# First pair of an attention kernel: k and q turned by TensorE through PSUM and copied out, where DMA transpositions stood

## The chip, the cores and the metric

One core of a Trainium2 chip runs the program alone. The metric is the device time of one execution in microseconds (us); the median of several executions is compared. TensorE is called PE below, VectorE DVE, ScalarE ACT, GpSimd POOL, and SP is the engine from whose queue every DMA of this kernel is issued.

## What is computed

```python
def _attn_ref(q, k, v):                       # 8 batches, 8 heads, 1152 rows, 64 columns
    q_pool = q.reshape(B, H, S // 2, 2, D).mean(axis=3)
    scores = scale * np.matmul(q_pool, k.transpose(0, 1, 3, 2))
    scores = scores - np.max(scores, axis=-1, keepdims=True)
    attn = np.exp(scores)
    attn = attn / (np.sum(attn, axis=-1, keepdims=True) + 1e-09)
    return np.matmul(attn, v)

def _moe_ref(x, w_in, w_out):                 # x: 4608 x 512, from the heads side by side
    h = x @ w_in                              # 512 x 2048
    g = h * np.cos(h)
    return g @ w_out                          # 2048 x 512
```

Neighbouring rows of q are averaged, attention runs over 576 pooled queries and 1152 keys a head, and its output goes through a feed-forward layer with the gate h cos(h).

## The kernel before, in words

The 64 heads are worked as 32 pairs. A pair's k is loaded, split into a high and a low float16 part side by side (`prep_k`: a cast on ACT, a subtraction on DVE for pair 0, on POOL later), and turned so that the 2 x 64 columns lie on the partitions (`transpose_k`, line 737, tile `k1`). The upper half of `k1` is copied by DMA into `k2` (`copy_k`, line 746), whose lower half is a constant. The pooled q goes the same way: its high part, written twice, is `q1s`, turned into `q1T`; its low part with the row's negative maximum beside it is `qs2`, turned into `q2T`. Scores are two matmuls each, `k1` with `q1T` and `k2` with `q2T`, so the maximum has to be known first: the main passes (`first_main` for pair 0, `head_main` for pairs 1 and 2, `mx_main` later) are matmuls whose only use is a DVE reduction to row maxima, `mxs`.

Pair 0 has steps of its own, `first_pair`: k in two halves of 9 blocks (one a head), q in two parts of 4 and 6 blocks of 128 columns (lines 1012 to 1020), eight main passes of 1024 columns, four for each head, the rests, then `first_q2` for each half: reduce to the maximum `m` (line 990), write it into `qs2` on ACT (line 991), turn 4 or 5 blocks (line 994). After that the score units begin (`s_unit`, line 1217, in the PSUM tile `st`), each with an exponential on ACT (line 1267, tile `pp`) and a product with v on PE (line 1342 for the first pairs).

Beside the pairs run the weights of the feed-forward layer: 16 slices, each loaded, decoded on DVE by three instructions of 1024 columns (lines 518, 521, 524), squared and scaled on ACT and split on POOL. The feed-forward matmuls (line 1553) can begin once the first eight slices are done and the first batch's attention output is there; from then on they fill PE between the pairs' work.

The order on each engine is not the order of the text. `arrange` takes all recorded instructions, gives each an estimated cost and due time, plays them through and fixes one order for each engine, which the chip then executes in that order. Matmuls named `warm` (60 of 128 columns, `fillers`, line 613) do no work of the result; they are given due times by `FILL`, start, end and spacing in the planner's time, and stand between the first pair's matmuls. `marks` and `held` tie the issue of some loads behind other DMAs: pair 1's k and q and the first v behind the mark "kT", later ones behind "q2T".

Of the kernel before, what the change touches and what calls it, by code (L numbers as in the profile page):

```python
# [10 lines left out]
F16 = mybir.dt.float16  # L11
# [9 lines left out]
P = 128  # L21
# [35 lines left out]
VACT = 6  # L57
WACT = (1, 0)
HB = 2 * WACT[0]
FILL = (14.0, 26.0, 0.2)  # L60
FREM = 5
NHW = 3
HS = (-16, -15, -14, -13, -12, -10, -12, -11, -10, -9, -8, -7, -7)
# [287 lines left out]
def tile_attention_ffn(  # L351
# [10 lines left out]
    nc = tc.nc  # L362
# [11 lines left out]
    KT = S // P  # L374
# [12 lines left out]
    HALF = (slice(0, D), slice(D, P))  # L387

    fix = ctx.enter_context(tc.tile_pool(name="fix", bufs=1))
# [3 lines left out]
    psum = ctx.enter_context(tc.tile_pool(name="psum", bufs=1, space=PSUM))  # L393

    k2 = [fix.tile([P, 2 * KT * P], F16, name=f"k2_{i}") for i in range(2)]
    qs2 = fix.tile([P, NSL, P], F16, name="qs2")
    nc.gpsimd.memset(qs2, 0.0)
    q1s = fix.tile([P, NSL + 1, 2, D], F16, name="q1s")
# [45 lines left out]
            pow2_of(dst, am)  # L444

    ident = fix.tile([P, P], BF16, name="ident")

    def make_ident():
        full = sb1.tile([P, QT * P], F32, tag="xo", name="full")[:, :P]
        nc.gpsimd.memset(full, 0.0)  # L450
        nc.gpsimd.affine_select(
            out=full,
            in_=full,
            compare_op=ALU.not_equal,
            fill=1.0,
            base=0,
            pattern=[[-1, P]],
            channel_multiplier=1,
        )
        nc.scalar.copy(ident, full)  # L460

    make_ident()

    def spread(dst, mx):
# [10 lines left out]
    marks = {}  # L475
# [134 lines left out]
    def fillers():  # L610
        t = psum.tile([P, 512], F32, tag="avb", name="warm")
        for k in range(int((FILL[1] - FILL[0]) / FILL[2])):
            mm = nc.tensor.matmul(
                t[:, 0:P], ident, ident, start=True, stop=True, skip_group_check=True
            )
            fill[mm.ins.name] = FILL[0] + FILL[2] * k

# [5 lines left out]
    k1 = [fix.tile([P, 2 * KT * P], F16, name=f"k1_{i}") for i in range(3)]  # L623
# [24 lines left out]
    kst, kld, qld, q1T, q2T, vld, vam, mxs = {}, {}, {}, {}, {}, {}, {}, {}  # L648
# [8 lines left out]
    def qs2_of(n):  # L657
        return qs2b if n < NHW and n % 2 else qs2
# [28 lines left out]
    def prep_k(n, us):  # L687
        if n not in kst:
            if n in ES:
                ks = w2[0].rearrange("p f e -> p (f e)")[:, ES[n] * 2 * KW : (ES[n] + 1) * 2 * KW]  # L690
                kst[n] = ks.rearrange("p (u a d) -> p u a d", a=2, d=D)
            else:
                kst[n] = sb1.tile([P, 2 * KT, 2, D], F16, tag="kst", name="kst")
        kv, ks = kld[n][:, us], kst[n][:, us]
        nc.scalar.copy(ks[:, :, 0], kv)  # L695
        (nc.gpsimd if n else nc.vector).tensor_sub(ks[:, :, 1], kv, ks[:, :, 0])  # L696
# [20 lines left out]
    def transpose_q1(n):  # L717
        t = sb1.tile([P, NSL + 1, P], F16, tag="q1T", bufs=3, name="q1T")
        tr = nc.sync.dma_start_transpose(t, q1s.rearrange("p s a d -> p (s a d)"))
        marks.setdefault("q1T", tr)  # L720
        q1T[n] = t

    def prep_q2(n):
# [11 lines left out]
    def transpose_k(n, us):  # L735
        cs = slice(us.start * P, us.stop * P)
        tr = nc.sync.dma_start_transpose(
            k1[n % 3][:, cs].rearrange("p (u c) -> p u c", c=P),
            kst[n][:, us].rearrange("p u a d -> p (u a d)"),
        )  # L740
        if us.stop == 2 * KT:
            marks.setdefault("kT", tr)

    def copy_k(n, us=KALL):
        cs = slice(us.start * P, us.stop * P)
        nc.sync.dma_start(k2[n % 2][HALF[0], cs], k1[n % 3][HALF[0], cs])


    mx_n = [0]
# [6 lines left out]
    def mx_main(n, t, c):  # L756
        if n not in mxs:
            mxs[n] = sb2.tile([P, NSL, 3], F32, tag="mxs", name="mxs")
        mx_n[0] += 1
        two = n < NMXF and mx_n[0] % 2  # L760
        banks, m = first_tile(2, None if two else "mx")
        last = None
        for h in range(2):
            last = after(
                nc.tensor.matmul(  # L765
                    banks[h],
                    q1T[n][:, h * QT + t, :],
                    kmain(n, k1[n % 3], c, h),
                    start=True,
                    stop=True,  # L770
                    skip_group_check=True,
                ),
                last,
            )
        if two:
            for h in range(2):
                nc.vector.reduce_max(mxs[n][:, h * QT + t, c : c + 1], banks[h], axis=AX.X)
        else:
            nc.vector.reduce_max(mxs[n][:, t : t + QT + 1 : QT, c], m, axis=AX.X)  # L779
# [125 lines left out]
    def head_q2(h):  # L905
        return lambda n: n < NHW and first_q2(h, n)
# [79 lines left out]
    def first_q2(h, n=0):  # L986
        ss = slice(0, QT) if h == 0 else slice(QT, NSL)
        qq = qs2_of(n)
        m = sb2.tile([P, NSL], F32, tag="m", bufs=1, name="m")
        nc.vector.reduce_max(m[:, ss], mxs[n][:, ss], axis=AX.X)  # L990
        nc.scalar.activation(qq[:, ss, D], m[:, ss], AF.Copy, scale=-1.0 / MDIV)
        if h == 0:
            q2T[n] = sb1.tile([P, NSL, P], F16, tag="q2T", bufs=2, name="q2T")
        tr = nc.sync.dma_start_transpose(
            q2T[n][:, ss], qq[:, ss].rearrange("p s c -> p (s c)")
        )
        if h == 1:
            marks.setdefault("q2T", tr)
            mxs.pop(n)

    def first_q1(ss):
        qt = qld[0]
        qs = qt[:, ss, 0, :]
        nc.vector.tensor_add(qs, qs, qt[:, ss, 1, :])
        mains = slice(ss.start, min(ss.stop, 2 * QT))
        parts = [(slice(0, P), mains, mains)]
        for h in range(2 if ss.stop > 2 * QT else 0):
            parts.append((HALF[h], slice(2 * QT, NSL), slice(2 * QT + h, 2 * QT + h + 1)))
        for ps, a, b in parts:
            src = qt[ps, a, 0, :]  # L1010
            src = src.unsqueeze(2).broadcast_to([src.shape[0], src.shape[1], 2, D])
            nc.scalar.copy(q1s[ps, b], src)
        if ss.start == 0:
            q1T[0] = sb1.tile([P, NSL + 1, P], F16, tag="q1T", bufs=3, name="q1T")
        cs = slice(ss.start, NSL + 1 if ss.stop == NSL else ss.stop)
        tr = nc.sync.dma_start_transpose(
            q1T[0][:, cs], q1s[:, cs].rearrange("p s a d -> p (s a d)")
        )
        if ss.start:
            marks.setdefault("q1T", tr)  # L1020

    def first_low(ss):
        qt = qld[0]
# [9 lines left out]
    def first_pair():  # L1033
        k_steps(0, 0)
        first_q1(QHEAD[0])
        constants()
        first_low(QHEAD[0])
        first_q1(QHEAD[1])
        k_steps(0, 1)
        copy_k(0, KHEAD[0])  # L1040
        load_v(0)
        first_low(QHEAD[1])
        qld.pop(0)
        nc.gpsimd.memset(qs2b, 0.0)
        for t in range(QT):
            first_main(0, t, ("st", "mx")[t % 2])
        first_rest(0, "st")
        first_q2(0)
        copy_k(0, KHEAD[1])
        v_max_begin(0)  # L1050
        first_v()
        prep_v(0)
        for t in range(QT):
            first_main(1, t, ("mx", None)[t % 2])
        first_rest(1, None)
        mx_mixed(0)
        first_mixed_rest()
        first_q2(1)
# [6 lines left out]
    def transpose_q2(n):  # L1065
        t = sb1.tile([P, NSL, P], F16, tag="q2T", bufs=2, name="q2T")
        tr = nc.sync.dma_start_transpose(t, qs2.rearrange("p s c -> p (s c)"))
        marks.setdefault("q2T", tr)
        q2T[n] = t

    def load_v(n):
# [39 lines left out]
    def prep_v_lo(n, hs):  # L1111
# [3 lines left out]
        for h in hs if nf < KT else ():  # L1115
# [6 lines left out]
                ALU.subtract,  # L1122
            )

    def mains(c, ts):
        def fn(n):
            for t in ts:
                mx_main(n, t, c)

        return fn  # L1130

    def k_steps(n, part):
        us = KCUT[part] if n else KHEAD[part]
        if n == 0:
            prep_k(n, us)
        elif part == 0:
            prep_k(n, KALL)
        transpose_k(n, us)

# [4 lines left out]
        (-2, 1, pool_q),  # L1144
        (-2, 2, prep_q1),
        (-2, 2, transpose_q1),
        (-2, Q2AT, prep_q2),
        (-2, 3, lambda n: k_steps(n, 1)),
        (-2, 4, late(mains(0, (0,)))),
        (-2, 5, late(mains(0, (1,)))),  # L1150
        (-1, 2, copy_k),
        (-2, 6, late(mains(0, (2,)))),
        (-2, 7, late(mains(0, (3,)))),
# [8 lines left out]
        (-1, 3, late(mx_mixed_rest)),  # L1162
        (-1, 3, late(m_write)),
        (-1, 4, late(transpose_q2)),
        (HS[0], head_main(0, 0)),
        (HS[1], head_main(0, 1)),
# [22 lines left out]
    st = {}  # L1189
# [613 lines left out]
    for u in range(NUNITS):  # L1803
        p, i = divmod(u, NU)
# [12 lines left out]
        while credit > 0.0:  # L1817
            c = next(ffn, None)
# [74 lines left out]
```

## Time and profile before

| | |
|---|---|
| median of 3 runs | 1529.35 us (1526.34 to 1531.48) |
| the profiled execution, its own time | 1525.26 us |
| its span, first to last instruction | 1523.4 us |
| outside the span | 1.86 us |
| instructions | 39324 |

The profile's page gives the busy time of each engine over the span. The other views used below are the timeline (instructions of one engine in order of time, neighbours of one kind merged; the brackets give idle time just before and what ended it), the table by stretches (busy time of each engine within a stretch) and the table of waits (who waited for whom).

### The profile page before, as it was taken

To read this page: it belongs to the slowest core of one execution; us is meant where nothing else is said; L and a number is where in the kernel's file an instruction comes from. 1 tells how busy PE (TensorE), PEld (TensorE's weight loads), DVE (VectorE), ACT (ScalarE), POOL (GpSimd) and SP (SyncE) were. 2 spreads that over 40 slices of the span, in tenths; PEclk is the share of its full clock that TensorE was granted. 3 is DMA by queue.
4 is the path that set the end of the run, shared out by engine and by line. 5 is a ranking of instruction groups with operands and counts; after the bars stand their busy time and mean duration, and the time that the engine had idled before them with its cause. 6 is when DMAs were issued, how large, how long until landed. Compare 5 with 4: busy or idle time off the path is not lost.

```text
span 1523.4 us, 39324 instructions
## 1 busy us (share of the span) xinstructions
PE 1490.2 (98%) x16774; PEld 1027.2 (67%) x16774; DVE 1124.1 (74%) x1556; ACT 1172.4 (77%) x1475; POOL 929.6 (61%) x806
## 2 busy tenths in 40 slices
PE   5999999999999999999999999999999999999998
PEld 3777787657666676666666657667666667666665
DVE  7898987777888788887867887878787875343332
ACT  4877689888988788887968887988888787864442
POOL 4644757886665858686555586676767665521222
PEclk9999999999999999999999999999999999999999
DMA  9978742635354433535333334454453321001000
GB/s 264 273 219 181 177 93 48 125 78 116 70 102 102 108 89 76 128 79 123 73 75 79 73 83 107 86 104 103 80 120 83 80 56 32 17 19 32 20 16 22
DMA packets 226111, 145.15 MB, mean 95 GB/s; under 512 B 202448, under 2 KB 204752, under 8 KB 223888
## 3 DMA queue, kind: packets, MB, share of 16 engines
q1 hardware_dynamic: 225936, 142.65, 40.5%
q8 instruction: 131, 2.15, 0.6%
q14 instruction: 44, 0.36, 0.1%
HBM read 74.45 MB, written 10.49 MB: 56 GB/s over the span
## 4 chain that ended last, share of the span: by engine, by line
PE 88%; DVE 5%; ACT 3%; issue 1%; DMA 1%; POOL 1%; SPq 0%; ACTq 0%; DVEq 0%; POOLq 0%
PE f L1553 20%; PE f L1613 19%; PE st L1217 15%; PE ava L1293 8%; PE avb L1293 6%; PE m L765 6%; PE st L1240 2%; PE mx L1613 1%; DVE mxs L779 1%; PE ava L1342 1%; PE st L1553 1%; PE mx L808 1%; PE mx L787 1%; PE avb L1553 1%; PE mx L1553 1%
## 5 line engine op out<-in xcount | busy, mean ns | idle before, releaser
L1279 POOL TENSOR_TENSOR pp<-e,pp 128x512 f16<-128x512 f32 x374 | 457.3, 1244 | 270.6 <-ACT pp L1273 141.9
L1553 PEld LDWEIGHTS <-w 128*128 128x128 f16 x3456 | 331.4, 98 | 61.7 <-issue 3.0
L1553 PE MATMUL f<-xT,w 128*128 128x256 f16 x3048 | 366.2, 273 | 0.3 <-DVE y L1581 0.2
L1267 ACT ACTIVATE e<-st 128x1024 f32<-128x1024 f32 x267 | 272.5, 1020 | 109.9 <-PE st L1217 84.1
L779 DVE TENSOR_REDUCE mxs<-m 128x2 f32<-128x1024 f32 x232 | 283.2, 1221 | 97.1 <-PE m L765 95.0
L1613 PE MATMUL f<-w,g 128*128 128x512 f16 x1440 | 333.2, 380 | 0.7 <-DVE y L1581 0.7
L1503 POOL TENSOR_TENSOR g<-hsc,g 128x512 f16<-128x512 f32 x144 | 192.0, 1355 | 162.1 <-ACT g L1502 160.4
L1273 ACT CAST pp<-e 128x1024 f16<-128x1024 f32 x267 | 278.9, 1045 | 9.8 <-PE ava L1293 2.1
L1293 PEld LDWEIGHTS <-pp 128*128 128x128 f16 (+1 forms) x7062 | 238.8, 100 | 64.2 <-issue 12.5
L1613 PEld LDWEIGHTS <-g 128*128 128x128 f16 x1680 | 158.5, 98 | 177.3 <-DVE y L1581 0.9
L1217 PE MATMUL st<-q1T,k 128*128 128x512 f16 x576 | 218.8, 380 | 4.4 <-ACT pp L1267 4.1
L1293 PE MATMUL ava<-vc,pp 128*128 128x65 f16 (+5 forms) x4502 | 218.9, 198 | 1.3 <-DVE lx L1407 1.2
L1217 PE MATMUL st<-q2T,k 128*128 128x512 f16 x576 | 218.5, 379 | 0.0
L1293 PE MATMUL avb<-vc,pp 128*128 128x65 f16 (+1 forms) x3052 | 179.3, 197 | 0.0
L1217 PEld LDWEIGHTS <-k 128*128 128x128 f16 x1152 | 104.8, 98 | 100.9 <-issue 11.2
L1491 DVE TENSOR_TENSOR hsc<-hsc,y 128x512 f32<-128x512 f32 x144 | 134.8, 976 | 25.3 <-ACT y L1485 25.1
L1577 ACT ACTIVATE hsc<-f,small 128x512 f32<-128x512 f32 x127 | 86.7, 683 | 83.6 <-PE f L1553 83.2
L1581 DVE SCALAR_TENSOR_TENSOR y<-f,r1a,y 128x512 f32<-128x512 f32 x127 | 94.6, 745 | 66.1 <-ACT y L1580 61.3
L765 PE MATMUL m<-k,q1T 128*128 128x512 f16 x464 | 138.1, 379 | 2.5 <-DVE mxs L779 2.0
L1275 DVE TENSOR_TENSOR pp<-e,pp 128x1024 f16<-128x1024 f32 x80 | 127.5, 1593 | 16.7 <-ACT pp L1273 16.2
L1502 ACT CAST g<-hsc 128x512 f16<-128x512 f32 x144 | 83.0, 613 | 11.6 <-PE f L1613 11.6
L696 POOL TENSOR_TENSOR kst<-kld,kst 128x1152 f16<-128x1152 f32 x30 | 75.5, 2516 | 20.9 <-ACT kst L695 20.9
(189 smaller groups left out, 1853.6 us busy)
## 6 DMA issues: line engine op xcount, KB each, us to landing
vld<-in_v_dram SPq DMA_DIRECT2D x32, 576.0 KB, 3.8
kld<-in_k_dram SPq DMA_DIRECT2D x30, 576.0 KB, 4.5
qld<-in_q_dram SPq DMA_DIRECT2D x30, 576.0 KB, 4.6
k<-k SPq DMA_DIRECT2D x31, 288.0 KB, 3.5
wraw<-in_moe_w_in_dram SPq DMA_DIRECT2D x8, 1024.0 KB, 8.0
wraw<-in_moe_w_out_dram SPq DMA_DIRECT2D x8, 1024.0 KB, 6.1
out_dram<-ob SPq DMA_DIRECT2D x32, 256.0 KB, 2.4
left<-lx SPq DMA_DIRECT2D x64, 16.0 KB, 2.0
```

What stands on the lines that cost most here:

```text
L765: nc.tensor.matmul(banks[h], q1T[n][:, h * QT + t, :], kmain(n, k1[n % 3], c, h), start=True, stop=True, skip_group_check=True,),
L779: nc.vector.reduce_max(mxs[n][:, t : t + QT + 1 : QT, c], m, axis=AX.X)
L1217: nc.tensor.matmul(s[:, y, :].rearrange("p (t c) -> p t c", c=P), kcol(p, w, j, h), x[:, h * QT : (h + 1) * QT, :], start=part == 0, stop= ...
L1267: nc.scalar.activation(e, s, AF.Exp, scale=exp_scale, bias=l_add)
L1273: nc.scalar.copy(pp[:, 0, c0:n], e[:, c0:n])
L1275: nc.vector.tensor_sub(pp[:, 1, c0:n], e[:, c0:n], pp[:, 0, c0:n])
L1279: nc.gpsimd.tensor_sub(pp[:, 1, c], e[:, c], pp[:, 0, c])
L1293: mm = nc.tensor.matmul(out, w, x, start=start, stop=False, skip_group_check=True)
L1491: nc.vector.tensor_mul(hj, hj, y[:, j : j + 2])
L1503: nc.gpsimd.tensor_sub(gt[:, 1], hj, gt[:, 0])
L1553: mm = nc.tensor.matmul(ps[:, fi, :], w1[wt][:, hp, fs], ck.xT[hp][:, xi, cs], start=n == 0, stop=n == 3 * HP - 1, skip_group_check=True,)
L1613: nc.tensor.matmul(po, gt[:, gi, f % 2, ts_], w2[wt][:, f, :], start=f == 0 and (gi, wt) == (0, 0), stop=f == NF - 1 and (gi, wt) == (1, 0),)
```

## The change

Pair 0's four kinds of DMA transposition (k in two halves, q1 in two parts, q2 in two parts: 9, 9, 4, 6, 4 and 5 blocks, 37 in all) become PE transpositions of 128 columns against a float16 unit matrix `flip` into PSUM, with copies by ACT or DVE from there into the same SBUF tiles. The first half of k goes through the tile `st`, the second through two tiles `f`, q through `ava` (one tile, used four times). `KTURN` and `QTURN` say which engine copies which blocks: of k's halves ACT takes 5 blocks and DVE 4 each; of q1 DVE takes the 4 blocks and ACT the 6; of q2 DVE the 4 and ACT the 5. `FILL` begins and ends 6 earlier in the planner's time. The mark "kT" is now the first half's copy to `k2`, and "q2T" is the transposition of a later pair's q1. Later pairs keep their DMA transpositions.

```diff
-FILL = (14.0, 26.0, 0.2)
+FILL = (8.0, 20.0, 0.2)
+QTURN = (0, 1)
...
+    flip = fix.tile([P, P], F16, name="flip")
...
+        nc.scalar.copy(flip, full)
         nc.scalar.copy(ident, full)
...
     def transpose_q1(n):
...
-        marks.setdefault("q1T", tr)
+        marks.setdefault("q2T", tr)
...
-        nc.sync.dma_start(k2[n % 2][HALF[0], cs], k1[n % 3][HALF[0], cs])
+        cp = nc.sync.dma_start(k2[n % 2][HALF[0], cs], k1[n % 3][HALF[0], cs])
+        if n == 0:
+            marks.setdefault("kT", cp)
+
+    def turned(dst, src, tag, copies):
+        n = src.shape[1] // P
+        w = 2048 if tag == "st" else 1024
+        t = psum.tile([P, w], F16, tag=tag, bufs=2 if tag == "f" else 1, name="turn")
+        for i in range(n):
+            cs = slice(i * P, (i + 1) * P)
+            nc.tensor.transpose(t[:, cs], src[:, cs], flip)
+        for eng, a, b in copies:
+            cs = slice(a * P, b * P)
+            (nc.scalar.copy if eng else nc.vector.tensor_copy)(dst[:, cs], t[:, cs])
...
-        tr = nc.sync.dma_start_transpose(
-            q2T[n][:, ss], qq[:, ss].rearrange("p s c -> p (s c)")
-        )
+        src = qq[:, ss].rearrange("p s c -> p (s c)")
+        if n == 0:
+            dst = q2T[n][:, ss].rearrange("p s c -> p (s c)")
+            turned(dst, src, "ava", ((h, 0, src.shape[1] // P),))
+        else:
+            tr = nc.sync.dma_start_transpose(q2T[n][:, ss], src)
...
-        tr = nc.sync.dma_start_transpose(
-            q1T[0][:, cs], q1s[:, cs].rearrange("p s a d -> p (s a d)")
-        )
...
+        src = q1s[:, cs].rearrange("p s a d -> p (s a d)")
+        dst = q1T[0][:, cs].rearrange("p s c -> p (s c)")
+        turned(dst, src, "ava", ((QTURN[ss.start > 0], 0, src.shape[1] // P),))
...
+    KTURN = (
+        (("st", 0, KT, ((1, 0, 5), (0, 5, KT))),),
+        (("f", 0, 5, ((1, 0, 5),)), ("f", 5, KT, ((0, 0, KT - 5),))),
+    )
...
             prep_k(n, us)
-        elif part == 0:
+            for tag, a, b, copies in KTURN[part]:
+                cs = slice((us.start + a) * P, (us.start + b) * P)
+                turned(
+                    k1[0][:, cs],
+                    kst[0].rearrange("p u a d -> p (u a d)")[:, cs],
+                    tag,
+                    copies,
+                )
+            return
+        if part == 0:
             prep_k(n, KALL)
         transpose_k(n, us)
```

The planner makes new orders out of this. On DVE, from the pooling of q to the first half's maximum, this stood before (`w_1_84` is a weight slice, `m_132` to `m_152` the main passes in PSUM):

```order
L1004 TENSOR_TENSOR qld<-qld 128x5x64
L696 TENSOR_TENSOR kst<-kld,kst 128x9x64
L518 TENSOR_SCALAR w_1_84<-wraw 128x1024
L521 SCALAR_TENSOR_TENSOR w_1_84<-wraw,w_1_84 128x1024
L524 SCALAR_TENSOR_TENSOR w_1_84<-wraw,w_1_84 128x1024
L934 TENSOR_REDUCE mxs<-m_132 128x1
L934 TENSOR_REDUCE mxs<-m_137 128x1
L934 TENSOR_REDUCE mxs<-m_142 128x1
L934 TENSOR_REDUCE mxs<-m_147 128x1
L955 TENSOR_REDUCE mxs<-m_152 128x4
L990 TENSOR_REDUCE m<-mxs 128x4
```

and this stands now:

```order
L1022 TENSOR_TENSOR qld<-qld 128x5x64
L762 COPY q1T<-turn 128x512
L762 COPY k_0_94<-turn 128x512
L699 TENSOR_TENSOR kst<-kld,kst 128x9x64
L950 TENSOR_REDUCE mxs<-m_169 128x1
L762 COPY k_0_94<-turn 128x512
L950 TENSOR_REDUCE mxs<-m_174 128x1
L950 TENSOR_REDUCE mxs<-m_179 128x1
L950 TENSOR_REDUCE mxs<-m_184 128x1
L971 TENSOR_REDUCE mxs<-m_189 128x4
L1006 TENSOR_REDUCE m<-mxs 128x4
```

Three copies have come in, the third between the first and the second reduction, and the decoding of the first weight slice has left this place: it now stands behind the second half's main passes.

On PE the second main pass of the first head was followed before by one filler and the third pass; now the second half of k is turned between them, behind nine fillers and ahead of six (one row shown of each run of equal rows):

```order
L939 MATMUL m_174<-k_0_94,q1T 128x512
L616 LDWEIGHTS ident
L616 MATMUL warm<-ident 128x128
...
L759 LDWEIGHTS kst
L759 MATMUL turn<-flip,kst 128x128
...
L616 MATMUL warm<-ident 128x128
L939 LDWEIGHTS q1T
L939 MATMUL m_179<-k_0_94,q1T 128x512
```

The whole first half of k (9 blocks) and all of q1 (10 blocks) stand ahead of the first main pass.

On ACT, from the first v to the fifth exponential, this stood before:

```order
L1083 ACTIVATE vc_75,mxa<-vld 128x18x64
L695 CAST w_0_83<-w_0_83 128x18x64
L991 ACTIVATE qs_71<-m 128x4
L1106 ACTIVATE vc_75<-vld,sv 128x18x64
L712 CAST q1s<-w_0_83 128x1024
L712 CAST q1s<-w_0_83 64x128 x2
L1267 ACTIVATE pp<-st 128x1024
L991 ACTIVATE qs_71<-m 128x5
L1083 ACTIVATE vc_76,mxa<-vld 128x18x64
L1267 ACTIVATE pp<-st 128x1024
L531 ACTIVATE w_0_81,wmx<-w_1_84 128x4x256
L1267 ACTIVATE pp<-st 128x1024
```

and this stands now:

```order
L1121 ACTIVATE vc_75<-vld,sv 128x18x64
L1296 ACTIVATE pp<-st 128x1024
L715 CAST q1s<-w_0_83 128x1024
L715 CAST q1s<-w_0_83 64x128 x2
L1296 ACTIVATE pp<-st 128x1024
L1098 ACTIVATE vc_76,mxa<-vld 128x18x64
L1296 ACTIVATE pp<-st 128x1024
L1007 ACTIVATE qs_71<-m 128x5
L762 COPY q2T<-turn 128x640
L534 ACTIVATE w_0_81,wmx<-w_1_84 128x4x256
L698 CAST kst<-kld 128x18x64
L1296 ACTIVATE pp<-st 128x1024 x2
```

The first exponential (L1267, now L1296) has moved ahead of pair 1's q cast (L712, now L715), three of them now stand ahead of the second half's maximum (L991, now L1007), and the fourth stands behind a weight's square and the cast of pair 2's k.

## Rows read from the trace of the kernel before

**Rows 1.** The page, busy time of each engine over the span and its share.

```profile
PE 1490.2 (98%) x16774; PEld 1027.2 (67%) x16774; DVE 1124.1 (74%) x1556; ACT 1172.4 (77%) x1475; POOL 929.6 (61%) x806
```

**Rows 2.** The table by stretches: us, busy us and count of each engine, PEclk, DMA, GB/s.

```profile
30.00:190.00 160.00, 151.38 (x1448) 117.70 (x1448) 144.85 (x226) 115.98 (x151) 91.97 (x91) 1.00 0.83 216
190.00:1480.00 1290.00, 1283.63 (x14951) 873.32 (x14950) 948.53 (x1289) 1030.50 (x1284) 811.34 (x668) 1.00 0.36 79
```

**Rows 3.** Timeline of SP: start, us, queue, line, DMA (issue alone).

```profile
5.14 1.86 SPq L737 DMA_TRANSPOSE k<-kst  x1
...
13.46 0.57 SPq L667 DMA_DIRECT2D w<-in_k_dram  x1
...
22.06 0.39 SPq L1074 DMA_DIRECT2D vld<-in_v_dram  x1
22.90 4.30 SPq L737 DMA_TRANSPOSE k<-w  x2
27.29 1.37 SPq L719 DMA_TRANSPOSE q1T<-q1s  x1
```

**Rows 4.** Timeline of ACT, first 27 us.

```profile
5.48 0.62 ACT L1012 CAST q1s<-qld 128x512 f16<-128x512 f32 x1 [1.16 <-DVE qld L1004]
6.58 1.14 ACT L1012 CAST q1s<-qld 128x512 f16<-128x512 f32 x3 [0.48 <-DVE qld L1004]
7.74 0.67 ACT L695 CAST kst<-kld 128x576 f16<-128x576 f32 x1
...
19.27 1.15 ACT L695 CAST w<-w 128x1152 f16<-128x1152 f32 x1 [0.78 <-DMA w<-in_k_dram]
20.33 0.21 ACT L991 ACTIVATE qs<-m 128x4 f16<-128x4 f32 x1
...
26.46 1.02 ACT L1267 ACTIVATE pp<-st 128x1024 f32<-128x1024 f32 x1 [0.63 <-PE st L1217]
```

**Rows 5.** Timeline of DVE, first 33 us.

```profile
8.44 0.78 DVE L696 TENSOR_TENSOR kst<-kld,kst 128x576 f16<-128x576 f32 x1 [1.90 <-ACT kst L695]
...
13.81 3.55 DVE L934 TENSOR_REDUCE mxs<-m 128x1 f32<-128x1024 f32 x3
...
18.77 0.68 DVE L955 TENSOR_REDUCE mxs<-m 128x4 f32<-128x512 f32 x1
19.55 0.17 DVE L990 TENSOR_REDUCE m<-mxs 128x4 f32<-128x12 f32 x1
...
20.72 1.22 DVE L934 TENSOR_REDUCE mxs<-m 128x1 f32<-128x1024 f32 x1
...
27.53 0.17 DVE L990 TENSOR_REDUCE m<-mxs 128x5 f32<-128x15 f32 x1
27.61 0.70 DVE L518 TENSOR_SCALAR w<-wraw 128x1024 uint32<-128x1024 uint32 x1
...
29.61 1.23 DVE L524 SCALAR_TENSOR_TENSOR w<-wraw,w 128x1024 uint32<-128x1024 uint32 x1
32.21 1.29 DVE L867 TENSOR_REDUCE mxs<-m 128x1 f32<-128x512 f32 x2 [1.38 <-PE m L852]
```

**Rows 6.** Timeline of PE, first 32 us.

```profile
12.04 1.89 PE L923 MATMUL m<-k,q1T 128*128 128x512 f16 x4 [12.04 <-DMA q1T<-q1s]
...
15.89 0.84 PE L613 MATMUL warm<-ident 128*128 128x128 bf16 x6
...
21.13 0.67 PE L613 MATMUL warm<-ident 128*128 128x128 bf16 x9
...
28.39 1.90 PE L1342 MATMUL ava<-vc,pp 128*128 128x65 f32 x16
31.79 1.04 PE L852 MATMUL m<-k,q1T 128*128 128x512 f16 x4 [1.50 <-DMA q1T<-q1s]
```

**Rows 7.** The table of waits, 30 to 190 us, PE and DVE.

```profile
PE st L1217 <- ACT pp L1267: 3.6, 7, 1.1
...
DVE mxs L779 <- PE m L765: 4.4, 7, 1.1
```

More of the change, by code (lines that the diff above doesn't have):

```diff
@@ L993, in first_q2 @@
             q2T[n] = sb1.tile([P, NSL, P], F16, tag="q2T", bufs=2, name="q2T")
-        tr = nc.sync.dma_start_transpose(
-            q2T[n][:, ss], qq[:, ss].rearrange("p s c -> p (s c)")
-        )
+        src = qq[:, ss].rearrange("p s c -> p (s c)")
[4 more added lines that the diff above has]
+            tr = nc.sync.dma_start_transpose(q2T[n][:, ss], src)
         if h == 1:
-            marks.setdefault("q2T", tr)
             mxs.pop(n)
@@ L1015, in first_q1 @@
         cs = slice(ss.start, NSL + 1 if ss.stop == NSL else ss.stop)
-        tr = nc.sync.dma_start_transpose(
-            q1T[0][:, cs], q1s[:, cs].rearrange("p s a d -> p (s a d)")
-        )
-        if ss.start:
-            marks.setdefault("q1T", tr)
+        src = q1s[:, cs].rearrange("p s a d -> p (s a d)")
+        dst = q1T[0][:, cs].rearrange("p s c -> p (s c)")
+        turned(dst, src, "ava", ((QTURN[ss.start > 0], 0, src.shape[1] // P),))
     def first_low(ss):
@@ L1067, in transpose_q2 @@
         tr = nc.sync.dma_start_transpose(t, qs2.rearrange("p s c -> p (s c)"))
-        marks.setdefault("q2T", tr)
         q2T[n] = t
```

## The prediction, made before the changed kernel ran

> **What bounds the kernel now.** I read the page first, then the table by stretches, then the timelines of the first 33 us engine by engine, then the waits. PE is busy 98% of the span [rows 1], so almost all of the time is PE's work, and a change can win only from PE's idle time. The stretches say where that lies [rows 2]: from 190 to 1480 us PE is busy 1283.6 of 1290, 6.4 us idle; from 30 to 190 it is busy 151.4 of 160, 8.6 us idle. The largest single piece is the start: the first matmul begins at 12.04 and the wait in front of it ends with the DMA that turned q1 [rows 6]. That is the wait the change is aimed at.
>
> Two more things have to be seen. First, between 30 and 190 us DVE is busy 144.9 of 160 [rows 2]: this is the stretch in which the weights are decoded beside the pairs' maxima, and DVE has hardly more slack than PE. Second, the waits there run more often towards PE than towards DVE: PE lost 3.6 us to exponentials, while DVE lost 4.4 us in one group alone, waiting for PE's main passes [rows 7].
>
> **The change, part by part.** I follow the new order with the durations of before. Loads land when they did; k's first half is ready at 5.1, when its DMA transposition was issued [rows 3].
>
> *Turning k and q1.* A transposition of 128 columns on PE is not in the trace; nearest is a filler, of the same shape. Six fillers early take 0.84 us, nine later 0.67 [rows 6], and four main matmuls take 1.89 early, 1.04 later: PE stands at its lower level of 1.2 GHz at first and at 2.4 GHz by 21 us (the clock column says 1.00 for both stretches of rows 2). I use 0.11 a block and 0.43 a main matmul until 20 us; both ends are priced below. Nine blocks of k take from 5.15 to 6.3. ACT has cast q's first part by 6.10 [rows 4], four blocks of q follow to 6.75.
>
> *Copies.* No copy from PSUM stands in the trace. For DVE the nearest is a reduction of 512 columns from PSUM, 0.68 [rows 5]; for ACT, a cast of 576 columns at 0.67 and an exponential of 1024 from PSUM at 1.02 [rows 4] give 0.72 for 640 columns. The lower bound is nothing where an engine idles, the upper one 1.2 a copy, the reduction of 1024 [rows 5]. ACT's copy of k takes 6.3 to 7.05 and stands ahead of q's second part, whose three casts (1.14) end at 8.2 and the cast of k's second half (0.67) at 8.9 instead of 8.41 [rows 4]. DVE's subtraction behind it (0.78) ends at 9.7 instead of 9.22 [rows 5]: the copies delay the second half of k by 0.5. DVE's first two copies fall in idle time (1.90 us of it stands ahead of 8.44 [rows 5]) and cost nothing themselves.
>
> *First half's maxima.* PE turns q's last six blocks by 8.45, when the last cast is there, and its first main pass gives DVE a first reduction at 9.7, against 13.81. Not all of these 4.1 us stay: DVE had used the time before 13.81 to decode a weight slice. Now its third copy stands between the first and second reductions and waits for nine blocks that PE turns only after four main matmuls (8.45 to 10.2), nine fillers (to 11.1) and its own 1.1: 12.3. DVE idles from 10.9 to 12.3, copies to 13.0, then reduces three passes in 3.55 [rows 5], the last a little late because PE's fillers hold back its main pass, to 16.8; the rests (0.68) and the maximum end at 17.7, against 19.72. The gain here is 2.0 us.
>
> *q2 and the first score unit.* The maximum goes through ACT (0.21 [rows 4]) to 17.95, but on PE two pieces of the second half's passes and eleven fillers stand ahead of q2's four blocks, which end at 19.7; DVE idles about 1 us and copies to 20.4. A main matmul, seven fillers and the score unit's four matmuls follow; the first exponential begins near 21.7, against 26.46 [rows 4]: 4.8 earlier.
>
> *Second half.* From 20.72 to 27.70 DVE needed 6.98 us [rows 5]; it now starts at 20.4 and has one piece of decoding (0.70) in between, so the maximum stands at 28.1, 0.4 later than before. The other two pieces of decoding follow to 30.6, then pair 1's passes, which began at 32.21 after 1.38 us of idle time.
>
> *Pair 1's data.* The first loads behind the mark "kT" no longer queue behind four transpositions on SP; pair 1's k is issued at about 9.3 instead of 13.46 [rows 3]. Its turn comes later, though, since the second load of v (22.06) stands ahead of it and waits for ACT to have finished with the first; that is about 20.05, so k goes at 20.6 against 22.90, q1 4.3 us behind it at 24.9 against 27.29, landing 4.5 later [rows 3, 6]: 29.4.
>
> *Where both stand.* PE begins pair 1's passes at 29.4 instead of 31.79, having done four score units instead of two score units and one product with v (1.90 [rows 6]); two units are eight main matmuls at 0.22, 1.7, so that is the same work, and PE leads by **2.4 us**. DVE begins them at 30.6 instead of 32.21, but has decoded one slice where two were done before, and a slice is 3.2 us, 27.61 to 30.84 [rows 5]: it lags by **1.6 us**. The lag is the copies (four at 0.68 are 2.7, two of them in idle time) and the two new waits. POOL loses nothing on this path: it does the same subtractions earlier.
>
> *The clock.* At the higher level from 14 us on, PE would turn q2 a microsecond sooner and DVE would lag by about 0.6; at the lower one into the second half, the lag stays 1.6 or a little more. The Trainium skill (TensorE: Matmul & The Clock Gate, Part 4: PE-mode transpose) says that transpositions on PE do not count as activity for its clock as matmuls do, which speaks against this change; no run here shows it yet. By that rule the lower level lasts and the sum is the 1.6 I used; if transpositions counted, it would be about 0.6.
>
> *The sum.* From 30 to 190 us the two engines take turns at being last. Were PE alone the limit, 2.4 us would stay; were DVE, 1.6 us would be lost. The waits lean to PE, DVE's idle 15.1 us against 8.6, so I take 1.0 us of gain. What follows after 190 us is PE's own work. The profiled execution took 1525.26, so 1524.3; it lies 4.1 below the median of the runs shown, and my forecast for a median is 1529.35 less 1.0, **1528.4 us**.
>
> **The rivals.** A measurement of this kernel can tell about 0.3%, 4.6 us, from no change.
>
> *The start carries through.* The first exponential is 4.8 us earlier, and the DMA queue is rid of 37 blocks in a stretch in which PE twice waited for a transposition [rows 6]. If DVE's lag is taken up by its idle time and pair 1's data come sooner than I have them, the 4.8 stay, plus up to 1.5 from the second of those waits: 1523 to 1524.6. For it: DVE's waits for PE [rows 7]. Against it: DVE's 90% from 30 to 190 us.
>
> *DVE becomes the limit.* Nothing in the new order lets DVE catch up: the weights must be decoded before the feed-forward matmuls can fill PE, and each slice is later. With copies at their upper bound (two more times 0.5), the waits for k's and q2's blocks longer by 1 us each, and the fourth exponential standing on ACT behind a weight's square and the cast of pair 2's k, whose load has to land first, the lag grows from 1.6 to about 5, and PE, out of other work, idles for it: 1534. It decides once the lag exceeds what DVE can recover from its waits for PE, 4.4 us in their largest group. For it: the DVE row of the stretch [rows 2]. Against: most of DVE's idle time there is waiting for PE.
>
> *The wait was hidden anyway.* If DVE, busy decoding from 10.4 to 13.8 while the first passes waited, was the true limit of the start, nothing changes but the order: 1529.4. This differs too little from my forecast to be told apart and shares its chance.
>
> **How the numbers follow.** About the same, my forecast and the hidden wait together, 0.56; the start carries through 0.22; DVE the limit 0.22. These are also the chances of within 0.3%, faster and slower. The new order of the whole program adds some microseconds either way in each case, since PE's idle time up to 190 us falls differently. The range takes the faster case down to 1521.5 (its 1523 and 1.5 for the spread) and the slower one up to 1536 (its 1534 and 2 for the spread, as the runs shown go 2.1 above their median).
>
> **What would show it.** Right: first transposition on PE near 5.2, first main pass near 8.5, first reduction near 9.7, an idle gap of about 1.4 us on DVE behind it, first exponential near 21.7, pair 1's passes near 29.5, and more PE idle time from 30 to 190 us than 8.6. Wrong: copies from PSUM well off 0.7 us; pair 1's data landing before 27 or after 31; PE's idle time from 30 to 190 us unchanged (then the lead stays and it is the first rival), or grown by more than 5 us (then the second).

## The result, and the profile after

The changed kernel took 1540.22 us (median of 4 runs, 1538.25 to 1542.83) against 1529.68 for the kernel before beside it: a ratio of 1.0082, 95% interval 1.0056 to 1.0108. It is slower by 10.5 us by the medians. The forecast was 1528.4 in a range up to 1536. The profiled execution took 1541.73 us, its span is 1539.7. The two profiles lie further apart than the medians: that of before was taken of an execution 4.4 us below the 1529.68, this one 1.5 above its median, so of the 16.3 us between the spans some 6 are spread from run to run.

The head of the program did what the change is for. ACT's timeline of the changed kernel (columns as in [rows 4]; line 762 holds the copies from PSUM, line 1296 the exponentials) answers to [rows 4]:

```profile
6.49 0.69 ACT L762 COPY k<-turn 128x640 f16<-128x640 f16 x1 [0.25 <-PE turn L759]
8.81 0.79 ACT L762 COPY q1T<-turn 128x768 f16<-128x768 f16 x1
19.45 1.02 ACT L1296 ACTIVATE pp<-st 128x1024 f32<-128x1024 f32 x1 [0.77 <-PE st L1246]
```

The first exponential begins at 19.45, 7.0 us earlier. This is DVE's timeline of the changed kernel, where [rows 5] had the first reduction at 13.81, the maxima at 19.55 and 27.53 and pair 1's passes at 32.21:

```profile
6.94 0.42 DVE L762 COPY q1T<-turn 128x512 f16<-128x512 f16 x1
...
9.62 1.21 DVE L950 TENSOR_REDUCE mxs<-m 128x1 f32<-128x1024 f32 x1
11.59 0.42 DVE L762 COPY k<-turn 128x512 f16<-128x512 f16 x1 [0.76 <-PE turn L759]
...
16.10 0.17 DVE L1006 TENSOR_REDUCE m<-mxs 128x4 f32<-128x12 f32 x1
...
26.03 0.17 DVE L1006 TENSOR_REDUCE m<-mxs 128x5 f32<-128x15 f32 x1
...
28.58 1.29 DVE L883 TENSOR_REDUCE mxs<-m 128x1 f32<-128x512 f32 x2
```

PE's timeline of the changed kernel, which answers to [rows 6] (line 759 turns, line 939 has pair 0's main passes, line 868 pair 1's):

```profile
5.31 1.14 PE L759 MATMUL turn<-flip,kst 128*128 128x128 f16 x9 [5.31 <-DVE kst L699]
...
8.37 1.91 PE L939 MATMUL m<-k,q1T 128*128 128x512 f16 x4
...
10.89 0.67 PE L759 MATMUL turn<-flip,kst 128*128 128x128 f16 x9
...
11.72 0.59 PE L939 MATMUL m<-k,q1T 128*128 128x512 f16 x2
...
28.15 1.04 PE L868 MATMUL m<-k,q1T 128*128 128x512 f16 x4 [0.44 <-DMA q1T<-q1s]
```

At the start of pair 1 PE is 3.6 us ahead of its time before (28.15 for 31.79) and DVE also 3.6 us (28.58 for 32.21), though DVE has one weight slice less behind it (3.2 us by [rows 5]), which leaves it 0.4 us ahead. So the loss of 11 us comes later. The page's line of busy times answers to [rows 1]:

```profile
PE 1499.4 (97%) x16811; PEld 1032.5 (67%) x16811; DVE 1135.7 (74%) x1560; ACT 1176.8 (76%) x1480; POOL 930.9 (60%) x806
```

PE is busy 9.2 us longer than before for 37 more matmuls, and its span is 16.3 longer: 7.1 us are more idle time. The table by stretches (columns as in [rows 2]) says where:

```profile
30.00:190.00 160.00, 142.43 (x1293) 108.85 (x1291) 140.56 (x212) 104.84 (x139) 75.83 (x77) 0.95 0.75 200
190.00:1480.00 1290.00, 1282.13 (x15000) 875.73 (x14998) 958.75 (x1296) 1037.69 (x1291) 828.94 (x681) 1.00 0.35 80
...
60.00:70.00 10.00, 8.17 (x50) 5.95 (x49) 6.55 (x12) 7.57 (x13) 4.87 (x5) 0.83 0.91 321
90.00:100.00 10.00, 7.42 (x39) 4.79 (x38) 9.26 (x15) 6.19 (x8) 5.81 (x7) 0.83 0.94 259
...
130.00:140.00 10.00, 6.63 (x56) 3.90 (x55) 7.57 (x12) 5.78 (x10) 6.30 (x9) 0.68 0.97 183
...
180.00:190.00 10.00, 8.76 (x112) 7.00 (x111) 9.06 (x16) 4.34 (x5) 2.61 (x3) 0.83 0.67 123
```

From 30 to 190 us PE is now idle for 17.6 us instead of 8.6 [rows 2], DVE for 19.4 instead of 15.1: every engine does less there. And PE's granted clock is 0.95 instead of 1.00, with four dips. From 190 us on the two kernels are alike again. The table of waits, 30 to 190 us, answers to [rows 7] (line 781 main passes, 1246 score units, 1269 rests of the scores; columns: total, times, longest):

```profile
PE m L781 <- DVE mxs L795: 6.7, 5, 3.1
PE st L1246 <- ACT pp L1296: 6.1, 5, 1.8
PE st L1269 <- DMA q2T<-qs: 1.9, 1, 1.9
```

Before, no wait for an exponential or for DVE was longer than 1.1 us [rows 7], and the longest of all in this stretch was the 1.50 in front of pair 1's passes [rows 6]. Each dip of the clock lies behind such a wait, of 1.83, 1.45, 1.93 and 3.14 us; the wait of 1.37 at 56.75 has no dip behind it. This is PE's timeline of the changed kernel at that wait and at the first and the last of the four:

```profile
56.75 0.38 PE L1246 MATMUL st<-q1T,k 128*128 128x512 f16 x1 [1.37 <-ACT pp L1296]
...
59.77 0.59 PE L868 MATMUL m<-k,q1T 128*128 128x512 f16 x2
62.19 0.59 PE L1246 MATMUL st<-q1T,k 128*128 128x512 f16 x1 [1.83 <-ACT pp L1296]
62.57 0.63 PE L1246 MATMUL st<-q2T,k 128*128 128x512 f16 x1
63.00 0.63 PE L1246 MATMUL st<-q1T,k 128*128 128x512 f16 x1
...
181.24 0.91 PE L781 MATMUL m<-k,q1T 128*128 128x512 f16 x2 [3.14 <-DVE mxs L795]
```

The pair of main matmuls at 59.77 takes 0.59, the pair at 181.24 takes 0.91. A score matmul takes 0.38 at 56.75 and 0.63 at 62.57, and at the second place the next one follows after 0.43 us (62.57 to 63.00). What was late at the first place stands on ACT's timeline: the exponential that frees `st` is behind a cast, which waited for a DMA to be done with `kst`, and behind the cast of a weight.

```profile
59.12 1.15 ACT L698 CAST kst<-kld 128x1152 f16<-128x1152 f32 x1 [1.93 <-DMA k<-kst]
60.18 1.04 ACT L562 CAST w<-w 128x1024 f16<-128x1024 f32 x1
61.13 1.01 ACT L1296 ACTIVATE pp<-st 128x1024 f32<-128x1024 f32 x1
```

At the last place it is on DVE's timeline: the reduction that PE waits for is behind a weight's maximum and a cast of q of 2.33 us.

```profile
176.60 1.21 DVE L538 TENSOR_REDUCE wmx<-wf 128x1 bf16<-128x1024 f32 x1
177.73 2.33 DVE L717 CAST q1s<-qld 128x1024 f16<-128x1024 f32 x1
179.97 1.21 DVE L795 TENSOR_REDUCE mxs<-m 128x2 f32<-128x1024 f32 x1
```

None of these instructions is new and none belongs to pair 0. What changed is where they stand: the planner made another order for the whole stretch. The two orders, as the kernels of the experiments hold them, differ beyond it too, over the first 40% of PE's instructions.

### The profile page after: what moved, and what is told of

It reads as the page before. It is cut to its first block, busy times and chain, and to the rows that moved or that the text cites. A ratio compares the mean times of both kernels' runs of the same rounds, so it can differ in the third digit from the quotient of the medians.

```text
span 1539.7 us, 39394 instructions
## 1 busy us (share of the span) xinstructions
PE 1499.4 (97%) x16811; PEld 1032.5 (67%) x16811; DVE 1135.7 (74%) x1560; ACT 1176.8 (76%) x1480; POOL 930.9 (60%) x806
## 4 chain that ended last, share of the span: by engine, by line
PE 87%; DVE 7%; ACT 3%; DMA 2%; issue 1%; SPq 0%; ACTq 0%; DVEq 0%
PE f L1582 20%; PE f L1642 19%; PE st L1246 14%; PE ava L1322 8%; PE avb L1322 6%; PE m L781 6%; PE st L1269 2%; DVE q1s L717 2%; DVE mxs L795 1%; PE mx L1642 1%; PE ava L1371 1%; PE avb L1371 1%; PE st L1582 1%; PE mx L803 1%; PE mx L824 1%
## 5 line engine op out<-in xcount | busy, mean ns | idle before, releaser
L1308 POOL TENSOR_TENSOR pp<-e,pp 128x512 f16<-128x512 f32 x374 | 464.1, 1262 | 257.4 <-ACT pp L1302 127.5
L1296 ACT ACTIVATE e<-st 128x1024 f32<-128x1024 f32 x267 | 272.7, 1022 | 104.6 <-PE st L1246 84.3
L1304 DVE TENSOR_TENSOR pp<-e,pp 128x1024 f16<-128x1024 f32 x80 | 124.0, 1550 | 16.7 <-ACT pp L1302 16.2
```

Of the source, the lines that this page charges most:

```text
L1296: nc.scalar.activation(e, s, AF.Exp, scale=exp_scale, bias=l_add)
L1304: nc.vector.tensor_sub(pp[:, 1, c0:n], e[:, c0:n], pp[:, 0, c0:n])
L1308: nc.gpsimd.tensor_sub(pp[:, 1, c], e[:, c], pp[:, 0, c])
```

## The experiments

The theory after the result: the turning is a gain, and the new order of the later pairs' work costs more than it brings. In the expectations this is theory O. The rivals: the added PE work and copies cost the time (theory W); or the order of one queue alone does it; or the loss is a few single places.

All order experiments use one edit. The instructions common to both kernels are given the order of a list, in place of the planner's own; the list stands in the kernel as a table. Where a kernel has instructions that the list does not have (transpositions and copies, or DMA transpositions), they are put by hand behind a named neighbour.

```diff
     for e in engines:
         prev = None
-        for k in order[e]:
-            for i in nodes[k]["ins"]:
+        for i in given[e]:
```

**The changed work in the old order (turned_old_order).** `given` is the order of before; the 37 transpositions and their copies are put in where the data are ready.

> The changed program, its work untouched, but with every instruction that it shares with the kernel before in the order of the kernel before; PE's 37 transpositions and the copies are put in between by hand. Theory O (the new order from 30 to 190 us costs the time: PE waits behind misplaced work on ACT, DVE and SP, and its clock falls in the gaps): as fast as before, 1524 to 1531 us, PE idle from 30 to 190 us near 7 to 9 us, granted clock 1.00. Theory W (the copies and transpositions themselves, as added work, put DVE and ACT behind): stays at 1537 to 1543.

Measured: 1527.16 us against 1527.65 for before, ratio 0.9997 (0.9984 to 1.0010, 10 runs). The table by stretches of this run has PE at full clock and only 7.4 us idle:

```profile
30.00:190.00 160.00, 152.63 (x1461) 119.43 (x1462) 144.60 (x226) 116.41 (x153) 90.68 (x91) 1.00 0.80 213
```

So the added work costs nothing that can be measured. Nor does it win anything in this order: the first exponential is at 25.91 (26.46 before [rows 4]), because the old order keeps the decoding of a weight ahead of the first reductions.

**The old work in the new order (dma_new_order).** The kernel before, with its DMA transpositions, and `given` the order of the changed kernel.

> The converse: the program before, with its DMA transpositions, in the order of the changed kernel, the six transpositions put back into SP's queue at their old neighbours. Theory O: 1537 to 1546 us, PE idle from 30 to 190 us 15 us or more, granted clock under 1.00 there. Theory W: 1526 to 1532.

Measured: 1551.19 us, ratio 1.0156 (1.0134 to 1.0177, 4 runs). Its table by stretches:

```profile
30.00:190.00 160.00, 140.71 (x1215) 106.29 (x1214) 139.83 (x212) 104.62 (x141) 75.94 (x84) 0.95 0.75 204
```

No instruction is added or changed here and 23.5 us are lost. Idle time and clock are nearly those of the changed kernel. So an order alone can cost this much. The time is above the range of theory O too, and not all of it belongs to the order of the later pairs: this order was made for turned data, and with the DMA transpositions in it PE is busy for only 13.9 of the first 30 us, where the changed kernel has 19.2. In this order the turning itself is worth 11 us (1551.19 to 1540.22, the ratios 1.0156 and 1.0082 give the same).

**The new head, the old rest (turned_head_old_rest).** The changed kernel's order up to the planner's time 28, about the end of pair 0's maxima; behind it the order of before. As the rule by which the list was made:

```diff
-        given[e] = new[e]
+        head = [i for i in new[e] if start[i] < 28.0]
+        given[e] = head + [i for i in old[e] if i not in head]
```

> The changed program in its own order up to the end of the first pair's maxima (some 26 us), and from there on all that is left in the order of the kernel before. Theory O: what the head won stays, 1522 to 1529 us. Theory W: 1537 to 1543, since the same copies are made.

Measured: 1523.68 us, ratio 0.9981 (0.9968 to 0.9993, 10 runs): faster than before by 2.9 us by that ratio (1.1 to 4.9 by its interval) and 15.4 us below the changed kernel by the two ratios. It beats both kernels. Its timeline of PE at the start of pair 1 (line 907 has pair 1's passes here):

```profile
27.09 1.04 PE L907 MATMUL m<-k,q1T 128*128 128x512 f16 x4 [0.31 <-DMA q1T<-q1s]
```

PE begins them 4.7 us earlier than before [rows 6]. Its timeline of DVE, where pair 1's reductions begin at 30.98 with two weight slices done, as in the order of before:

```profile
30.98 1.28 DVE L922 TENSOR_REDUCE mxs<-m 128x1 f32<-128x512 f32 x2
```

Its table by stretches, with 7.9 us of idle time on PE, not 17.6:

```profile
30.00:190.00 160.00, 152.12 (x1451) 119.08 (x1451) 146.66 (x228) 116.10 (x153) 94.42 (x93) 0.99 0.77 209
```

This kernel has every instruction of the changed one, so the two profiles can be set against each other: its span is 1521.0 with PE busy for 1494.1, so 26.9 idle; the changed kernel's is 1539.7, with 1499.4 busy and 40.3 idle. Of the 18.7 us between them 13.4 are idle time and 5.3 are longer busy time of the same matmuls; the granted clock over the span is 0.994 in the changed kernel's profile and 0.999 in this one.

**How far the new order goes (cut60, cut100, cut150).** The same rule with 60, 100 and 150 in place of 28.

```diff
-        head = [i for i in new[e] if start[i] < 28.0]
+        head = [i for i in new[e] if start[i] < 150.0]
```

> The changed program in its own order up to the planner's time 60, from there on what is left in the order of the kernel before (turned_head_old_rest has this cut at 28 and took 1523.7). Theory O, with the loss spread over the four places where PE idles and its clock falls (near 61, 95, 134 and 178 us in the changed kernel): about 1 of the 4 lost, 1525 to 1529. If one place carries it all and it lies early: 1536 or more; if late: 1522 to 1525.

> The same with the cut at the planner's time 100. Loss spread: 2 of the 4, 1528 to 1533. One early place: 1536 or more; one late place: 1522 to 1526.

> The same with the cut at the planner's time 150. Loss spread: 3 of the 4, 1532 to 1537. One early place: 1538 or more; one late place: 1523 to 1528.

Measured: 1526.84 us, ratio 1.0002 (0.9988 to 1.0016); 1528.1, 1.0004 (0.9990 to 1.0018); 1533.86, 1.0036 (1.0007 to 1.0064). All three lie in the ranges for a loss that is spread, that of cut100 at the lower edge. The table by stretches of cut60, PE idle for 7.2 us:

```profile
30.00:190.00 160.00, 152.83 (x1443) 118.50 (x1442) 147.75 (x226) 115.37 (x151) 92.55 (x93) 0.98 0.76 208
```

That of cut100, PE idle for 11.4 us:

```profile
30.00:190.00 160.00, 148.61 (x1412) 115.60 (x1411) 146.71 (x224) 113.41 (x149) 88.20 (x88) 0.98 0.76 204
```

That of cut150, PE idle for 13.1 us:

```profile
30.00:190.00 160.00, 146.87 (x1350) 112.94 (x1350) 139.38 (x217) 108.21 (x143) 77.53 (x80) 0.96 0.73 198
```

With the full order at 1.0082 the loss grows with the part that is new: by the ratios about 3 us from 28 to 60, little up to 100, some 5 up to 150 and 7 behind that. The first of these steps is not sure, since the two intervals overlap and PE idles no longer at 60 (7.2 us) than at 28 (7.9). No single place makes the loss, and by these numbers three quarters of it lie beyond 100 us of the planner's time, after pair 0.

**SP alone in the old order (sp_old).** The changed kernel's order on PE, ACT, DVE and POOL; on SP the order of turned_head_old_rest.

```diff
+        given["SP"] = head_old_rest["SP"]
```

> The changed program in its own order on PE, ACT, DVE and POOL, and on SP alone, whose queue issues every DMA, what follows the first pair in the order of the kernel before. If the DMA queue's order (a copy and a transposition of k ahead of the q2 that PE waits for) makes the gaps: 1524 to 1532. If ACT and DVE make them: 1537 to 1545.

Measured: 1579.99 us, ratio 1.0349 (1.0321 to 1.0378). Both expectations missed. ACT's timeline of this run:

```profile
79.47 1.15 ACT L731 CAST kst<-kld 128x1152 f16<-128x1152 f32 x1 [12.11 <-DMA kld<-in_k_dram]
80.53 1.04 ACT L595 CAST w<-w 128x1024 f16<-128x1024 f32 x1
81.47 1.01 ACT L1335 ACTIVATE pp<-st 128x1024 f32<-128x1024 f32 x1
```

PE's timeline of the same run, at the score unit that needs this exponential done:

```profile
82.54 0.58 PE L1285 MATMUL st<-q1T,k 128*128 128x512 f16 x1 [11.74 <-ACT pp L1335]
```

It is the first of the four places, six times as large: the same cast of a later pair's k stands ahead of the same exponential, but now it waits for its load, which the other order of SP issues late, and PE waits 11.74 us. So this run makes a longer wait of its own and cannot tell whether SP's order alone makes the gaps of the changed kernel. What it shows is that one engine's order holds only together with the orders of the others.

**Another order without any turning (dma_hand).** The kernel before with one number of the planner changed, its estimate for handing on a result of ACT. The work is the same, the order another.

```diff
-HAND = {"PE": 0.21, "Activation": 0.08}
+HAND = {"PE": 0.21, "Activation": 0.1}
```

> The program before, nothing changed but one estimate of the planner (the hand-over time behind an ACT instruction, 0.10 in place of 0.08 us), which gives another order of the same work. Theory O says that the order before was a good one among many, so that another costs time without any change of work: 1532 to 1545 us. Theory W: 1526 to 1533.

Measured: 1532.69 us, ratio 1.0034 (1.0018 to 1.0049, 7 runs). The time lies in both ranges, so it does not decide between the theories. But the ratio is clear of 1: a change that has nothing to do with the first pair costs 5 us, so the planner's orders differ by that much on their own. It is not this stretch alone: PE idles 4.1 us longer than before over the span, 1.4 of them from 30 to 190 us and 2.7 behind.

**Mending single places (fix_act, fix_q2, fix_dve, fix_all).** The changed kernel in its own order with a few instructions moved: on ACT two exponentials ahead of what they stood behind, on DVE a reduction ahead of the cast, and for `q2T` a chain on three engines. One of the two swaps on ACT and the one on DVE, written as orders of instructions (the kernels hold them in the table):

```diff
+L1296 ACTIVATE pp
 L698 CAST kst
 L562 CAST w1
-L1296 ACTIVATE pp
...
 L538 TENSOR_REDUCE wmx
+L795 TENSOR_REDUCE mxs
 L717 CAST q1s
-L795 TENSOR_REDUCE mxs
```

> The changed kernel in its own order with two exponentials on ACT each moved ahead of the work that they stood behind: one ahead of the cast of a k that waits for a DMA (61 us) and one ahead of three weight scalings that wait for DVE (95 us). Theory A (the loss lies in single places at which a late instruction makes PE idle, and in the slow matmuls behind it): the waits of 1.8 and 1.5 us go, with some 2 us of slow matmuls behind them; 2 to 6 us faster than the changed kernel's 1540.2, so 1534 to 1538. Rival B (ACT and DVE are as late at the next place, so that a wait only moves): 1539 to 1542.

> The changed kernel in its own order with the chain to one q2T (130 us) moved ahead: on DVE the five instructions up to the maximum ahead of one reduction of a weight, on ACT the writing of qs ahead of one exponential, on SP the transposition of q2T ahead of a copy and a transposition of k. Theory A: the wait of 1.9 us goes, with about 1 us behind it: 1 to 3 us faster than 1540.2, so 1537 to 1539. Rival B: 1539 to 1542.

> The changed kernel in its own order with one swap on DVE: a reduction of a main pass (180 us) ahead of the cast of q1s of 2.3 us. Theory A: of the wait of 3.1 us 2 go, with 1 us of slow matmuls behind it: 1.5 to 4 us faster than 1540.2, so 1536 to 1538.7. Rival B: 1539 to 1542.

> The three edits together. Theory A: their gains add up, 5 to 12 us faster than 1540.2, so 1528 to 1535, with PE idle from 30 to 190 us for under 12 us instead of 17.6. Rival B: 1538 to 1542, with other waits of the same sum in that stretch.

Measured, beside a kernel before of 1528.2: 1538.16 us, ratio 1.0063 (1.0041 to 1.0086); 1541.69, 1.0093 (1.0067 to 1.0119); 1542.95, 1.0105 (1.0080 to 1.0130); all three together 1534.12, 1.0051 (1.0032 to 1.0069). In the expectations theory A is that single places make the loss, and rival B that a mended wait only moves. The first lies between the two. The second and the third won nothing that can be measured, against theory A; the third is above the range of rival B too. On PE's timeline of fix_act the wait of 1.83 us at the mended place is gone (62.28), but the exponential before it, with 1.37 and no slow matmuls in the changed kernel's profile, is now waited for 1.77 us, and slow matmuls follow:

```profile
57.19 0.58 PE L1285 MATMUL st<-q1T,k 128*128 128x512 f16 x1 [1.77 <-ACT pp L1335]
57.57 0.63 PE L1285 MATMUL st<-q2T,k 128*128 128x512 f16 x1
...
62.28 0.38 PE L1285 MATMUL st<-q1T,k 128*128 128x512 f16 x1
```

The slow matmuls do not follow each such wait. On PE's timeline of fix_q2, at the same score unit:

```profile
56.27 0.38 PE L1285 MATMUL st<-q1T,k 128*128 128x512 f16 x1 [1.77 <-ACT pp L1335]
56.48 0.38 PE L1285 MATMUL st<-q2T,k 128*128 128x512 f16 x1
```

On PE's timeline of fix_dve, of the 3.14 us at the place that was mended 1.19 are left, with another wait for DVE close behind:

```profile
183.13 0.59 PE L820 MATMUL m<-k,q1T 128*128 128x512 f16 x2 [1.19 <-DVE mxs L834]
184.55 1.37 PE L1361 MATMUL ava<-vc,pp 128*64 128x65 f32 x36 [0.82 <-DVE lx L1475]
```

Yet the run is no faster: its span is 1545.3. (The profiled execution is the slowest of the four, 1547.34 us; the others took about 1543.) The table by stretches of this run, far ahead of the edit:

```profile
30.00:70.00 40.00, 38.06 (x299) 29.99 (x298) 31.51 (x50) 22.90 (x30) 17.11 (x16) 0.85 0.89 256
```

The order there is the changed kernel's own, yet the granted clock is 0.85; the changed kernel's profile has 0.96 from 30 to 70 us. So the same order does not lose the same time in each run: the granted clock over the span is 0.993 to 0.997 in the changed kernel's four runs and 0.988 to 0.992 in the four of fix_dve. A mended place of 2 us can't be told from that. The three edits together win about 4.7 us by the ratios (1.0082 to 1.0051), but the two intervals overlap, so a gain is likely and its size is open. The waits of fix_all, 30 to 190 us:

```profile
PE m L820 <- DVE mxs L834: 7.0, 7, 1.7
PE st L1285 <- ACT pp L1335: 4.6, 5, 1.6
```

Its table by stretches:

```profile
30.00:190.00 160.00, 143.56 (x1351) 110.44 (x1350) 147.46 (x224) 111.37 (x147) 82.13 (x84) 0.99 0.75 200
```

The time is that of theory A, the idle time is that of rival B: PE still idles for 16.4 us (under 12 were expected), in more and shorter waits, none over 1.7. The granted clock of the stretch is 0.99, and over the span it was 0.999 in five of the eight runs (0.992 in the slowest, 1542.05 us). PE is busy 4.1 us less over the span than in the changed kernel (1495.3 by its page). So what went with these edits are the longest waits and a part of the work at the lower clock; the sum of the idle time in the stretch hardly moved. That the idle time is spread over the order is what the cuts show.

## Why the prediction was wrong

The mechanism of the head held, step by step, and its sizes were on the careful side:

| step | predicted | measured |
|---|---|---|
| first transposition, first main pass on PE | 5.2, 8.5 | 5.31, 8.37 |
| first reduction on DVE, idle time behind it | 9.7, 1.4 | 9.62, 0.76 |
| copies: DVE 512 columns, ACT 640 columns | 0.68, 0.72 | 0.42, 0.69 |
| first half's maximum done, first exponential | 17.7, 21.7 | 16.27, 19.45 |
| second half's maximum done | 28.1 | 26.20 |
| pair 1's transposition of q1 issued | 24.9 | 24.61 |
| pair 1's passes, PE and DVE | 29.4, 30.6 | 28.15, 28.58 |

*The clock.* I assumed the lower level until 20 us. Nine blocks at 5.31 take 1.14 us, nine at 10.89 take 0.67, and two main matmuls at 11.72 take 0.59, where four at 8.37 took 1.91, 0.43 apart: PE was at the higher level of 2.4 GHz some nine microseconds earlier than I had it. The work that it had done until then were 19 transpositions, four main matmuls and nine fillers. The Trainium skill (TensorE: Matmul & The Clock Gate, Part 4: PE-mode transpose) says that transpositions on PE do not count for its clock as matmuls do. By that rule, which I had weighed, the lower level would have lasted longer; the trace shows no sign of it here (1.14 to 0.67 for nine blocks), but no run separates the transpositions from the matmuls and fillers beside them.

*The step that failed* is the sum, with its two sentences "From 30 to 190 us the two engines take turns at being last" and "The new order of the whole program adds some microseconds either way in each case". I took the balance of that stretch from the kernel before and carried only the lead of PE and the lag of DVE into it. But that balance belongs to one order of some 2000 instructions, and the change replaced it. With the old order behind the new head (turned_head_old_rest) a part of the lead does arrive: 2.9 us of the 4.7 that PE is ahead there, where I had reckoned 2.4 for PE alone and taken 1.0. With the new order behind the same head it is lost, and 11 us more with it. I priced the term as noise of a few microseconds on either side; the runs show 15.4 us between two orders of the same instructions, 23.5 for before's own work in an order made for the turning, and 5 for a planner's number that I would have called harmless. The forecast of "no change" was thus a forecast for a kernel that was not built.

*The rivals.* "DVE becomes the limit" had the right sign and its test came true (PE's idle time grew by 9.0 us, more than 5). Its mechanism did not: DVE does not lag at pair 1 (0.4 us ahead, where I had it 1.6 behind), its copies are cheaper than I took them, and from 30 to 190 us it is busy for less time than before, 140.6 against 144.9 [rows 2]. PE's largest group of waits there is for DVE (6.7 us), but DVE in its turn waits 7.7 us for PE's main passes: that speaks for the order of the two and not for too much work on DVE. A part of it was right at another place: an exponential behind a cast that waits for its data holds PE up, at 61 us and not, as I had it, at the fourth exponential of the head. "The start carries through" is not what the changed kernel does. With the old order behind the head (turned_head_old_rest) the time falls within its 1523 to 1524.6, but by luck: the kernel before beside it took 1527.65, and the gain is 2.9 us, not 4.8.

*What could have been read.* The prediction weighs the first thirty microseconds of the new order and nothing behind them, though what PE waits for from 30 to 190 us is decided there: which cast stands ahead of which exponential can be seen in the order; how long it waits cannot.

*What stays open.* Why the planner arrives at a worse order was not tried, nor whether a change of its estimates would find a better one from the new head. Whether the new order of one engine alone carries the loss is not shown, since sp_old made a wait of its own and PE, ACT and DVE were not put back singly. Why the lower clock follows one wait and not another of the same length was not tried. The single places of the idle time that remains in fix_all were not mended one by one.

## What to carry to other kernels

Where one planner orders the whole program, an edit at the start is two edits: itself, and a new order for everything behind it. Separate them before judging either: give the changed kernel the old order behind the changed part. Here that turned a loss of 11 us into a gain of 3. A wait on an engine that is nearly always busy costs more than its length where the clock falls behind it: of the two orders here with nearly the same idle time in the stretch (17.6 us in the changed kernel, 16.4 in fix_all) the one with the shorter waits was likely the faster.

## What the runs showed of the hardware

- In the changed kernel's profile four waits of PE, of 1.83, 1.45, 1.93 and 3.14 us, were followed by matmuls at the lower level: score matmuls of 512 columns 0.43 us apart at 62.57 instead of 0.21 at 56.27 in fix_q2, with a granted clock of 0.68 to 0.83 over the ten microseconds. Not each such wait was: a wait of 1.77 us at one and the same score unit was followed by slow matmuls in fix_act and by quick ones in fix_q2. Between the changed kernel and turned_head_old_rest, with the same instructions, PE's busy time differs by 5.3 us.
- A copy of 512 float16 columns from PSUM takes DVE 0.42 us, less than the 0.68 of a reduction of 512 float32 columns [rows 5]; ACT takes 0.69 for 640.
